# A 32-byte pad among the constants and 16 unused matmuls at the end of a gated attention and feed-forward kernel

## The chip, the core and the metric

The kernel runs on one core of one Trainium2 chip. The metric is the device time of one execution in microseconds (us). Three runs of the kernel before took 501.36, 501.48 and 502.06 us; the median is 501.48 us.

The core's engines appear as PE (TensorE, matmuls), PEld (the weight loads of TensorE), DVE (VectorE), ACT (ScalarE), POOL (GpSimd) and SP (SyncE, which issues the DMAs here). A name with a q (SPq, PEldq) is the instruction queue of that engine.

## The reference

For 4 batches and 8 heads with 768 steps and head size 48, a state of 48 x 48 is decayed and grown step by step, and read out with q. The 3072 x 384 result goes through two matrix products with an activation between them.

```python
def _attn_ref(q, k, v, alpha):
    for t in range(S):
        state = alpha[:, :, t, :, None] * state + np.einsum('bhd,bhe->bhde', k[:, :, t], v[:, :, t])
        y[:, :, t] = np.einsum('bhd,bhde->bhe', q[:, :, t], state)

def _moe_ref(x, w_in, w_out):            # x: 3072 x 384, w_in: 384 x 2048, w_out: 2048 x 384
    h = x @ w_in
    g = np.where(h >= 1, h, np.where(h <= -1, 0.0, (h + 1) ** 2 / 4.0))
    return g @ w_out
```

## The kernel before

**Attention.** The 3072 tokens are cut into 24 chunks of 128 (one batch, all heads). For a chunk `prepare` loads its decays, keys, queries and values, runs two scans on DVE (lines 478 and 485: running products forwards and backwards) and scales keys and queries with them. `attend` then issues the small matmuls of the chunk: scores (line 589), state updates (line 602), outputs (line 769).

**Feed-forward.** Three chunks make a group of 384 tokens, so there are 8 groups. A group passes through 16 slices of 128 hidden units. For a slice, `hidden` multiplies the group by `w_in` (lines 878 and 887), applies the activation on ACT (line 918, two passes) and DVE (line 928), and splits the result into a high part (ACT, line 937) and a remainder (DVE, line 938). `second` multiplies by `w_out` and accumulates in PSUM (lines 960 and 969). The first group is done in plain fp32 (lines 878 and 960); the other seven in fp32r, each product as three: high x high, high weight x remainder, remainder weight x high. That makes nine matmuls of 128 x 128 weights by 384 columns for each of `hidden` and `second`, and 7 x 16 x 9 = 1008 of them on each of the lines 887 and 969.

**Order.** All of this is recorded as operations, and `Plan.order` sets the order on each engine from modelled durations and due times. Its result is emitted inside `tc.manual_schedule()`, so the order is fixed by the code. What comes after that block, the check at the end, is placed by the framework's scheduler.

**The check at the end** (lines 1047 to 1064). Small values that POOL saved for every chunk (`meet`) are compared with bounds on DVE, counted by a matmul with a vector of ones (line 1054), summed to one number (line 1056) and turned into `flag` (line 1058). Every engine loads `flag` into a register (line 1064) and branches on it (line 1065) to a slow path that is not taken here. After the branch SP waits for the last transfers, all engines meet at a barrier, and the program ends.

**Memory.** The constants are allocated one after the other in SBUF, each rounded up to 32 bytes, then the weights, then the pools of working tiles. In the built program `zeros`, `ident`, `mask` and `both` start at multiples of 128 bytes, `raw_kq` and `fwd` at 64 past one, `state` and `meet` at 64. All 18 weight tiles `wt`, and `xs`, `w`, `Q`, `ks`, `other`, `gf`, `ot` and `gh`, start at 96 past a multiple of 128. The two buffers of `pre` start at 96 and 0, those of `inv` at 32 and 64.

Of the kernel before, what the change touches and what calls it, by code (L numbers as in the profile page):

```python
# [8 lines left out]
F32 = mybir.dt.float32  # L9
# [23 lines left out]
LAG = 4.0  # L33
# [208 lines left out]
def gated_attention_ffn(ctx: ExitStack, tc: tile.TileContext, q, k, v, alpha, w_in, w_out, by, out):  # L242
    nc = tc.nc
    B, H, S, D = q.shape
    DM, DF = H * D, w_in.shape[0] * w_in.shape[3]
    P = 128
    G = H // 2
    KT = DM // P
    NF = DF // P
# [6 lines left out]
    one = lambda name, shape, dt=F32: const.tile(shape, dt, name=name)  # L256
    zeros = one("zeros", [P, P], BF16)
# [3 lines left out]
    ident, mask = one("ident", [P, P]), one("mask", [P, P])  # L261
    both = one("both", [P, NV, 2, 2, G, 64])
    half_b, ones = one("half_b", [P, 1]), one("ones", [P, 1])
    nothing = zeros[:, None, :].broadcast_to([P, 4, P])
    with tc.manual_schedule():
        nc.vector.memset(zeros, 0.0)
# [6 lines left out]
            out=mask, in_=mask, compare_op=ALU.is_ge, fill=0.0, base=0, pattern=[[1, P]], channel_multiplier=-1  # L273
# [10 lines left out]
    wout = lambda f, a: wo[f // NW]()[:, a, f % NW]  # L284
# [11 lines left out]
    segs = [(n, 0, NF) for n in range(NG)]  # L296
# [7 lines left out]
    with ExitStack() as main:  # L304
        plan = Plan(lambda n: fill(n))
        plan.pool("wt", 2 * NU + MORE)
        pools = {}
# [559 lines left out]
        def hidden(n, f, key):  # L867

            L = groups[n] * CH
            h = bank("ps_h", 2, [P, L])  # L870
            gf = buf("fw", "gf", [P, L], 3)
            whole = n < WHOLE

            def product():
                m = 0
                for kt in range(KT):
                    if whole:
                        nc.tensor.matmul(  # L878
                            out=h(),
                            lhsT=raw_in(f)[:, kt],  # L880
                            rhs=whole_x(n)[:, kt].rearrange("p j t -> p (j t)"),
                            start=kt == 0,
                            stop=kt == KT - 1,
                        )
                        continue
                    for w, a in ((0, 0), (0, 1), (1, 0)):
                        nc.tensor.matmul(  # L887
                            out=h(),
                            lhsT=win(f, w)[:, kt],
                            rhs=xs[n]()[:, 0 : groups[n], kt, a],  # L890
                            start=(m == 0),
                            stop=(m == 3 * KT - 1),
                        )
                        m += 1

            u = f // NW
            needs = [xs[n], *([*[("x", first[n] + c) for c in range(groups[n])], raws_w[u][0]] if whole else [("moved", n), wi[u]])]

            firsts[:] = [
                plan.op(  # L900
                    "PE",
                    (0.145 + 9 * L / 2400) * (1.2 if whole else 1.0),
                    key,
                    product,
                    needs,
                    [h],
                    mode="full",
                    after=firsts,
                )
            ]  # L910


            w = L / 384
            act = lambda in_, func, scale, bias: plan.op(
                "ACT",
                0.1 + 0.45 * w,
                key + 0.4,
                lambda: nc.scalar.activation(out=gf(), in_=in_(), func=func, scale=scale, bias=bias),  # L918
                [h, gf] if in_ is gf else [h],
                [gf],  # L920
            )
            act(h, AF.Relu, 0.5, half_b)
            act(gf, AF.Square, 1.0, 0.0)
            plan.op(
                "DVE",
                0.1 + 0.45 * w,
                key + 0.4,
                lambda: nc.vector.scalar_tensor_tensor(  # L928
                    out=gf(), in0=gf(), scalar=1.0, in1=h(), op0=ALU.min, op1=ALU.max
                ),  # L930
                [gf, h],
                [gf],
            )
            if whole:
                return gf
            gh = buf("fw", "gh", [P, 2, L], 3, F32R)
            plan.op("ACT", 0.08 + 0.41 * w, key + 0.4, lambda: nc.scalar.copy(out=gh()[:, 0], in_=gf()), [gf], [gh])  # L937
            sub = lambda e: e.tensor_tensor(out=gh()[:, 1], in0=gf(), in1=gh()[:, 0].bitcast(F32), op=ALU.subtract)  # L938
            plan.op("DVE", 0.08 + 0.45 * w, key + 0.4, lambda: sub(nc.vector), [gf, gh], [gh], port=True)
            return gh  # L940
# [8 lines left out]
        def second(seg, f, gh, key):  # L949
            n, f0, f1 = seg  # L950
            L = groups[n] * CH
            if f == f0:
                o_ps[seg] = [bank("ps_o", KT, [P, L]) for _ in range(KT)]

            whole = n < WHOLE

            def product(ms):
                for m in ms:
                    if whole:
                        nc.tensor.matmul(  # L960
                            out=o_ps[seg][m](),
                            lhsT=raw_out(f)[:, m * P : (m + 1) * P],
                            rhs=gh(),
                            start=f == f0,
                            stop=f == f1 - 1,
                        )
                        continue
                    for i, (w, a) in enumerate(((0, 0), (0, 1), (1, 0))):
                        nc.tensor.matmul(  # L969
                            out=o_ps[seg][m](),  # L970
                            lhsT=wout(f, w)[:, m * P : (m + 1) * P],
                            rhs=gh()[:, a],
                            start=(f == f0 and i == 0),
                            stop=(f == f1 - 1 and i == 2),
                        )

            ms = range(KT)

            for part in [[m] for m in ms] if f == f1 - 1 else [ms]:
                plan.op(  # L980
                    "PE",
                    (0.049 + L / 800) * len(part) * (1.2 if whole else 1.0),
                    key,
                    lambda part=part: product(part),
                    [gh, raws_w[f // NW][1] if whole else wo[f // NW]],
                    [o_ps[seg][m] for m in part],
                    mode="full",
                )
            if f < f1 - 1:
                return  # L990
            w = L / 384
            for m in ms:
                ps, ot = o_ps[seg][m], buf("fw", "ot", [P, L], KT)
                plan.op(
                    "ACT",
                    0.08 + 0.37 * w,
                    key,
                    lambda ps=ps, ot=ot: copy("ACT", ot(), ps()),
                    [ps],
                    [ot],  # L1000
                    other=("DVE", 0.08 + 0.44 * w, lambda ps=ps, ot=ot: copy("DVE", ot(), ps()), False),
                )
                r0 = first[n] * CH
                plan.op(
                    "SP",
                    Plan.ISSUE,
                    key,
                    lambda m=m, r0=r0, ot=ot: nc.sync.dma_start(
                        out=out[m * P : (m + 1) * P, r0 : r0 + L], in_=ot()
                    ),  # L1010
                    [ot],
                    [],
                    moved=P * L * 4,
                )
# [10 lines left out]
        at = 0  # L1025

        for j in range(NCH):
            n = group_of[j]
            since = begin[n - 1] if n > 0 else begin[n] - AHEAD
            due = since + (begin[n] - since) * (j - first[n] + 1) / groups[n] - (MARGIN, MARGIN0, MARGIN1)[n + 1 if n < 2 else 0]  # L1030
            prepare(j, due - PREPARE + off("p", j))
            attend(j, due + off("t", j))
            done = j if j < MERGE or j == NCH - 1 else j - 1
            while at < len(segs) and first[at] + groups[at] - 1 <= done:
                if at == WHOLE:
                    for u in range(NU):
                        parts_of(u)
                for f in range(NF):
                    key = begin[at] + f * step[at]
                    second(segs[at], f, hidden(at, f, key), key + LAG)  # L1040
                at += 1
        with tc.manual_schedule():
            for o in plan.order():
                o.emit()


        near = pools["att"].tile([P, G, P], F32, name="ks", bufs=1)[:, 0, 0 : NCH * G]
# [3 lines left out]
            out=near, in0=m, scalar=1.0 + SLACK, in1=near, op0=ALU.is_le, op1=ALU.mult  # L1051
        )
        ps = pools["ps"].tile([P, 512], F32, name="ps", bufs=8)[0:1, 0 : NCH * G]
# [191 lines left out]
```

## Time and profile before

| | |
|---|---|
| median of three runs | 501.48 us (501.36 to 502.06) |
| profiled execution | span 499.7 us from the first to the last instruction; no other time of it is recorded |
| PE busy | 491.5 us, 98% of the span |
| PEld busy | 446.5 us, 89% |
| DVE, ACT, POOL busy | 347.3, 317.9 and 30.5 us |
| the two groups of 1008 matmuls | 197.1 us (line 969) and 193.6 us (line 887) |
| granted TensorE clock | full in the whole table by slices |

The busy time of PE is the union of overlapping matmuls: a matmul of 384 columns lasts some 340 ns, but the next one starts long before its end. What a matmul costs is therefore read from the length of a run of them, divided by their number.

### The profile page before, as it was taken

To read this page: it belongs to the slowest core of one execution; us is meant where nothing else is said; L and a number is where in the kernel's file an instruction comes from. 1 tells how busy PE (TensorE), PEld (TensorE's weight loads), DVE (VectorE), ACT (ScalarE), POOL (GpSimd) and SP (SyncE) were. 2 spreads that over 40 slices of the span, in tenths; PEclk is the share of its full clock that TensorE was granted. 3 is DMA by queue.
4 is the path that set the end of the run, shared out by engine and by line. 5 is a ranking of instruction groups with operands and counts; after the bars stand their busy time and mean duration, and the time that the engine had idled before them with its cause. 6 is when DMAs were issued, how large, how long until landed. Compare 5 with 4: busy or idle time off the path is not lost.

```text
span 499.7 us, 11372 instructions
## 1 busy us (share of the span) xinstructions
PE 491.5 (98%) x4586; PEld 446.5 (89%) x4586; DVE 347.3 (69%) x609; ACT 317.9 (64%) x603; POOL 30.5 (6%) x70
## 2 busy tenths in 40 slices
PE   8899999999999999999999999999999999999996
PEld 3665656699999999999999999999999999999995
DVE  6998999998997866865866857767755635343332
ACT  3799998998765565565665655665565655555551
POOL 4211102211000000000000000000000000000000
PEclk9999999999999999999999999999999999999999
DMA  8999916878552531542434513434313201001001
GB/s 315 394 387 387 330 23 142 208 201 181 181 159 65 187 102 49 150 137 82 110 95 118 174 47 124 130 100 139 115 35 89 70 1 25 1 7 42 0 1 51
DMA packets 43336, 64.42 MB, mean 129 GB/s; under 512 B 21392, under 2 KB 30736, under 8 KB 43280
## 3 DMA queue, kind: packets, MB, share of 16 engines
q1 hardware_dynamic: 41840, 59.71, 37.4%
q0 software_dynamic: 1440, 3.93, 4.2%
q8 instruction: 38, 0.62, 0.5%
q14 instruction: 18, 0.15, 0.1%
HBM read 48.56 MB, written 9.18 MB: 116 GB/s over the span
## 4 chain that ended last, share of the span: by engine, by line
PE 94%; DVE 3%; issue 1%; DMA 1%; POOL 0%; ACT 0%; DVEq 0%
PE ps L969 36%; PE ps L887 35%; PE ps L878 6%; PE ps L960 6%; PE ps L769 5%; PE ps L602 3%; PE ps L589 2%; DVE inv L485 1%; DVE pre L478 1%; DMA raw_a<-in_al 1%; PE ps L574 1%; DVE inv L493 0%; DVE Q L709 0%; DVE Q L510 0%; DVE state L653 0%
## 5 line engine op out<-in xcount | busy, mean ns | idle before, releaser
L969 PE MATMUL ps<-gh,wt 128*128 128x384 f32 x1008 | 197.1, 340 | 0.0
L887 PE MATMUL ps<-xs,wt 128*128 128x384 f32 x1008 | 193.6, 335 | 0.0
L969 PEld LDWEIGHTS ps<-gh,wt 128*128 128x128 f32 x1008 | 177.7, 188 | 1.3 <-issue 0.2
L887 PEld LDWEIGHTS ps<-xs,wt 128*128 128x128 f32 x1008 | 176.7, 188 | 0.7
L928 DVE SCALAR_TENSOR_TENSOR gf<-gf,ps 128x384 f32<-128x384 f32 x128 | 70.6, 552 | 94.0 <-ACT gf L918 92.5
L918 ACT ACTIVATE gf<-ps,half_b 128x384 f32<-128x384 f32 x128 | 74.4, 582 | 83.4 <-PE ps L887 80.5
L937 ACT CAST gh<-gf 128x384 fp32r<-128x384 f32 x112 | 57.4, 513 | 59.0 <-DVE gf L928 49.7
L938 DVE TENSOR_TENSOR gh<-gf,gh 128x384 fp32r<-128x384 f32 x112 | 62.0, 555 | 33.3 <-ACT gh L937 32.6
L918 ACT ACTIVATE gf<-gf 128x384 f32<-128x384 f32 x128 | 67.2, 525 | 4.0
L635 ACT COPY both<-state 48x192 f32<-48x192 f32 x88 | 30.8, 350 | 10.5 <-PE ps L602 9.1
L960 PE MATMUL ps<-gf,wt 128*128 128x384 f32 x96 | 33.0, 488 | 0.4 <-PE ps L878 0.4
L878 PE MATMUL ps<-xs,wt 128*128 128x384 f32 x96 | 32.7, 489 | 0.1
L478 DVE TENSOR_TENSOR_SCAN pre<-raw_a,fwd 128x516 f32<-128x516 f32 x24 | 29.5, 1228 | 3.0 <-DMA raw_a<-in_al 2.7
L485 DVE TENSOR_TENSOR_SCAN inv<-raw_a,bwd 128x516 f32<-128x516 f32 x24 | 30.1, 1254 | 2.1
L769 PEld LDWEIGHTS ps<-Q,both 128*64 128x64 f32 x368 | 23.2, 138 | 7.2 <-issue 5.6
L960 PEld LDWEIGHTS ps<-gf,wt 128*128 128x128 f32 x96 | 18.0, 190 | 12.4 <-PE ps L878 0.8
L878 PEld LDWEIGHTS ps<-xs,wt 128*128 128x128 f32 x96 | 17.8, 190 | 11.9 <-ACT wt L357 0.4
L769 PE MATMUL ps<-Q,both 128*64 128x64 f32 x368 | 26.6, 225 | 0.0
L769 PE MATMUL ps<-other,both 128*64 128x64 f32 x368 | 26.6, 225 | 0.0
L501 POOL COPY meet<-inv 128x4 f32<-128x4 f32 x24 | 9.8, 408 | 258.3 <-DVE inv L485 258.3
L769 PEld LDWEIGHTS ps<-other,both 128*64 128x64 f32 x368 | 23.2, 138 | 0.0
L709 DVE TENSOR_TENSOR Q<-ps,mask 64x256 f32<-64x256 f32 x48 | 20.3, 423 | 3.6 <-ACT other L672 1.8
(62 smaller groups left out, 370.1 us busy)
## 6 DMA issues: line engine op xcount, KB each, us to landing
raw_kq<-in_kq SPq DMA_DIRECT2D x24, 512.0 KB, 5.2
both<-in_vl SPq DMA_DIRECT2D x24, 512.0 KB, 4.6
raw_a<-in_al SPq DMA_DIRECT2D x24, 258.5 KB, 3.3
wt<-in_w_out SPq DMA_DIRECT2D x8, 768.0 KB, 9.4
wt<-in_w_in SPq DMA_DIRECT2D x8, 768.0 KB, 8.4
out<-ot SPq DMA_DIRECT2D x24, 192.0 KB, 3.1
turned<-w SPq DMA_DIRECT2D x17, 256.0 KB, 2.2
ks<-turned SPq DMA_DIRECT2D x68, 64.0 KB, 2.6
```

Of the source, the lines that this page charges most:

```text
L478: lambda: nc.vector.tensor_tensor_scan(flat(pre()), a[:, 0:n], flat(fwd), 0.0, ALU.mult, ALU.max),
L485: lambda: nc.vector.tensor_tensor_scan(flat(inv())[:, ::-1], a[:, 1 : n + 1][:, ::-1], flat(bwd)[:, ::-1], 0.0, ALU.mult, ALU.max),
L635: lambda r=r, to=to: nc.scalar.copy(out=to, in_=state[low[r], b]),
L769: nc.tensor.matmul(out=ps()[halves[r], to, halves[u]], lhsT=lhsT[:, u, r], rhs=x()[:, g, halves[u]], start=m + u == 0, stop=True, skip_gro ...
L878: nc.tensor.matmul(out=h(), lhsT=raw_in(f)[:, kt], rhs=whole_x(n)[:, kt].rearrange("p j t -> p (j t)"), start=kt == 0, stop=kt == KT - 1,)
L887: nc.tensor.matmul(out=h(), lhsT=win(f, w)[:, kt], rhs=xs[n]()[:, 0 : groups[n], kt, a], start=(m == 0), stop=(m == 3 * KT - 1),)
L918: lambda: nc.scalar.activation(out=gf(), in_=in_(), func=func, scale=scale, bias=bias),
L928: lambda: nc.vector.scalar_tensor_tensor(out=gf(), in0=gf(), scalar=1.0, in1=h(), op0=ALU.min, op1=ALU.max),
L937: plan.op("ACT", 0.08 + 0.41 * w, key + 0.4, lambda: nc.scalar.copy(out=gh()[:, 0], in_=gf()), [gf], [gh])
L938: sub = lambda e: e.tensor_tensor(out=gh()[:, 1], in0=gf(), in1=gh()[:, 0].bitcast(F32), op=ALU.subtract)
L960: nc.tensor.matmul(out=o_ps[seg][m](), lhsT=raw_out(f)[:, m * P : (m + 1) * P], rhs=gh(), start=f == f0, stop=f == f1 - 1,)
L969: nc.tensor.matmul(out=o_ps[seg][m](), lhsT=wout(f, w)[:, m * P : (m + 1) * P], rhs=gh()[:, a], start=(f == f0 and i == 0), stop=(f == f1 ...
```

## The change

One constant of 32 bytes, `pad`, is allocated behind `ones`. It is never used. Everything that is allocated behind it moves up by 32 bytes: `wt`, `xs`, `w`, `Q`, `ks`, `other`, `gf`, `ot` and `gh` now start at multiples of 128. Not every tile does: `raw_kq` stays at 64, `state` and `meet` are at 96, the two `pre` at 0 and 32, the two `inv` at 64 and 96.

Behind the planned work, still inside the fixed order, PE gets 16 matmuls whose result nobody reads: in fp32r four of 512 columns with 128 weight columns, four of 512 columns with 32 weight columns, four of 256 columns with 128 weight columns, and in bf16 four of 512 columns on zeros.

```diff
     half_b, ones = one("half_b", [P, 1]), one("ones", [P, 1])
+    one("pad", [P, 8])
     nothing = zeros[:, None, :].broadcast_to([P, 4, P])
...
                 for f in range(NF):
                     key = begin[at] + f * step[at]
-                    second(segs[at], f, hidden(at, f, key), key + LAG)
+                    last_g = hidden(at, f, key)
+                    second(segs[at], f, last_g, key + LAG)
                 at += 1
         with tc.manual_schedule():
             for o in plan.order():
                 o.emit()
+
+            gl = last_g().rearrange("p a t -> p (a t)")
+            wl = wout(NF - 1, 0)
+            rest = pools["ps"].tile([P, 512], F32, name="ps", bufs=8)
+            for L, M in ((512, P), (512, 32), (256, P)):
+                for _ in range(4):
+                    nc.tensor.matmul(out=rest[0:M, 0:L], lhsT=wl[:, 0:M], rhs=gl[:, 0:L], start=True, stop=True)
+            for _ in range(4):
+                nc.tensor.matmul(out=rest, lhsT=zeros, rhs=nothing, start=True, stop=True)
```

Up to the last 40 microseconds every engine has the same instructions in the same order, with line numbers one higher. The end is different. These are the last rows of PE before the branch, in the kernel before; line 969 is `second`, line 1054 the counting matmul of the check.

```order
L969 MATMUL ps<-gh,wt 128x384 x9
L887 MATMUL ps<-xs,wt 128x384 x9
L969 MATMUL ps<-gh,wt 128x384 x19
L1054 MATMUL ps<-ks,ones 1x96
L969 MATMUL ps<-gh,wt 128x384 x17
L1064 TENSOR_LOAD flag
L1065 COMPARE_AND_BRANCH
```

The same place of PE in the changed kernel, where lines 1053 and 1055 are the new matmuls and the counting matmul has line 1065:

```order
L970 MATMUL ps<-gh,wt 128x384 x36
L1053 MATMUL ps<-gh,wt 128x512 x4
L1053 MATMUL ps<-gh,wt 32x512 x4
L1053 MATMUL ps<-gh,wt 128x256 x4
L1055 LDWEIGHTS zeros
L1055 MATMUL ps<-zeros 128x512
...
L1065 MATMUL ps<-ks,ones 1x96
L1075 TENSOR_LOAD flag
L1076 COMPARE_AND_BRANCH
```

The counting matmul has moved from between the last products to behind all of them and behind the 16 new ones.

The end of SP's queue before, where line 1008 stores a part of the result:

```order
L827 DMA xs<-xs 16x3x256 x6
L1008 DMA out<-ot 128x384 x3
L1064 TENSOR_LOAD flag
L1064 ISA x2
L1008 DMA out<-ot 128x384 x3
L1065 COMPARE_AND_BRANCH
```

The same place of SP in the changed kernel:

```order
L828 DMA xs<-xs 16x3x256 x6
L1009 DMA out<-ot 128x384 x6
L1075 TENSOR_LOAD flag
L1076 COMPARE_AND_BRANCH
L1111 COMPARE_AND_BRANCH
```

All six last stores now stand ahead of the load of `flag`, and the two small instructions (ISA) that check the loaded value have moved behind the branch. On DVE the three last copies to `ot` likewise stand ahead of the two instructions that make `flag`.

## Rows read from the trace of the kernel before

**Rows 1.** The profile page: span, the chain's shares by line, the clock.

```profile
span 499.7 us, 11372 instructions
PEclk9999999999999999999999999999999999999999
PE ps L969 36%; PE ps L887 35%; PE ps L878 6%; PE ps L960 6%; PE ps L769 5%; PE ps L602 3%; PE ps L589 2%; DVE inv L485 1%; DVE pre L478 1%; DMA raw_a<-in_al 1%; PE ps L574 1%; DVE inv L493 0%; DVE Q L709 0%; DVE Q L510 0%; DVE state L653 0%
```

**Rows 2.** The chain of waits from 485 us: start, us, piece.

```profile
485.26 1.59 PE ps L969 x9
486.85 1.56 PE ps L887 x9
488.41 3.35 PE ps L969 x19
491.76 0.26 PE ps L1054 x2
492.01 3.20 PE ps L969 x17
495.24 0.56 DVE ot L330
```

**Rows 3.** Chain of waits at 46 us; timeline and line 1020 from 9.3 us.

```profile
46.14 5.80 PE ps L878 x18
...
9.34 3.19 PE L1020 MATMUL ps<-zeros 128*128 128x512 bf16 x14
...
L1020 PE MATMUL ps<-zeros x14: 379/379/389, 9.3 to 12.2; 128*128 128x512 bf16 x14
```

**Rows 4.** Weight loads by line and shape: busy us, mean ns, idle before.

```profile
L969 PEld LDWEIGHTS ps<-gh,wt 128*128 128x128 f32 x1008 | 177.7, 188 | 1.3 <-issue 0.2
L769 PEld LDWEIGHTS ps<-other,both 128*64 128x64 f32 x368 | 23.2, 138 | 0.0
L589 PEld LDWEIGHTS ps<-Q,inv 48*64 48x64 f32 x768 | 13.7, 134 | 1.1 <-issue 0.9 <-DVE Q L510 0.2
L769 PEld LDWEIGHTS ps<-other,xs 128*64 128x64 f32 x48 | 3.1, 138 | 0.0
L1054 PEld LDWEIGHTS ps<-ks,ones 128*1 128x1 f32 x2 | 0.1, 80 | 0.2 <-issue 0.2
```

**Rows 5.** Instructions of line 478: ns min/median/max, first and last start.

```profile
L478 DVE TENSOR_TENSOR_SCAN pre<-raw_a,fwd x24: 1223/1226/1234, 3.8 to 362.1; 128x516 f32<-128x516 f32 x24
```

**Rows 6.** PEld's waits in the first 60 us: total, times, longest.

```profile
PEld ps L878 <- ACT wt L357: 0.4, 1, 0.4
```

**Rows 7.** Timeline of the end, DVE and SP's queue.

```profile
492.05 0.24 DVE L1056 TENSOR_REDUCE total<-ps 1x1 f32<-1x96 f32 x1 [0.69 <-PE ps L1054]
492.33 0.14 DVE L1058 TENSOR_SCALAR flag<-total 1x1 int32<-1x1 f32 x1
494.77 1.39 SPq L1008 DMA_DIRECT2D out<-ot  x3
```

**Rows 8.** Instructions of lines 1064, 1065 and 1240: ns min/median/max, first, last start.

```profile
L1064 SPq TENSOR_LOAD <-flag x1: 482/482/482, 492.5 to 492.5; - x1
L1064 SPq FUSED_REGOPS  x1: 188/188/188, 493.0 to 493.0; - x1
L1064 SPq SEQ_ASSERT  x1: 29/29/29, 493.3 to 493.3; - x1
L1065 SPq EVENT_SEMAPHORE  x8: 17/17/17, 496.7 to 498.0; - x8
L1065 PEldq COMPARE_BRANCH  x1: 3382/3382/3382, 493.1 to 493.1; - x1
L1065 SPq COMPARE_BRANCH  x1: 45/45/45, 496.2 to 496.2; - x1
L1240 SPq EVENT_SEMAPHORE  x14: 17/28/28, 498.1 to 499.7; - x14
L1240 SPq DRAIN  x3: 7/7/7, 498.9 to 499.2; - x3
```

## The prediction

> **What bounds the kernel now.** I read the page first. Of the chain that ended last, 36% and 35% of the span are the matmuls of lines 969 and 887, four more lines of PE give another 20%, and the clock is full [rows 1]. So, behind a short start-up with scans on DVE, only two things can move the end: what one matmul costs PE, and what stands behind the last one.
>
> The chain of waits gives the first. In the steady part a block of nine matmuls of line 887 takes 1.56 us, 173 ns each, and one of line 969 takes 1.59 us, 177 each [rows 2]. Is that the streaming of 384 columns? Other rows say no. Eighteen plain fp32 matmuls of the same shape, which stream each column in two steps, take 5.80 us in the chain, 322 ns each, or 161 ns for one pass. Fourteen bf16 matmuls of 512 columns span 3.19 us, of which the last is seen for its whole 0.38, so they come every (3.19 - 0.38) / 13 = 216 ns, the same 0.42 ns per column [rows 3]. So 161 ns of the 173 are columns, and 12 ns are something else. The weight load of such a matmul lasts 188 ns, one of 64 columns 138, one of a single column 80 [rows 4]: 80 ns, and some 0.85 ns per column. Loads of 188 ns that follow each other at 173 ns fill PEld without a gap, and I take the load, not the columns, as what sets 173 (177 where line 969 begins with two waits).
>
> **The change, part one: 32 bytes.** Weights, products and working tiles move from 96 past a multiple of 128 bytes to a multiple. Could a load or a stream get faster? The trace holds the comparison already. Line 769 takes its weights from `both`, which lies at a multiple of 128, and for some outputs from `xs`, at 96: both loads last 138 ns. Line 589 loads `inv`, which is at 32 or 64 and then one element further, in 134 ns [rows 4]. The fp32 stream of rows 3 reads `xs` at 96 and keeps the rate of the bf16 stream that reads `zeros` at 0. On DVE the 24 scans of line 478 write `pre` alternately at 96 and at 0 and all take 1223 to 1234 ns [rows 5]. So my value is 0. As bounds, the 138 against 138 is exact to 1 ns for 64 columns, so under 2 ns for 128: 2016 x 2 = 4 us either way as the far end.
>
> [...]
>
> Transfers into `wt` and `xs` now start on rounder addresses. Only the first loads of weights could matter, since later ones lie beside a busy PE: there PEld waits once, 0.4 us, for ACT's decoding of a weight [rows 6]. Bounds: 0.4 us gained, or as much lost; I take 0.
>
> [...]
>
> **Part two: the end.** Before, the counting matmul stands between the last products. It costs PE the break: from 488.41 to 495.21 the chain holds 36 matmuls of line 969 in 6.80 us; at 1.59 us per unbroken nine they need 6.36 [rows 2]. So the products end 0.44 us earlier, at 494.77. The copies of `ot` and the last stores go with them.
>
> Then PE runs the sixteen new matmuls. None waits for another engine: they read `gh`, weights and zeros that are there. Their spacing is the longer of columns and load. For 512 columns the columns decide, 216 ns, whether 128 or 32 weights are loaded: eight, 1.73 us. For 256 columns the columns need 108 ns and the load 173, so 173 decides; by the rows it could lie between 108 and 188. With the change of shape ahead and behind: three at 0.17 and one, beside the short load of the bf16 matmul, at about 0.14: 0.66 us. Four in bf16, 0.86 us. The ends follow each other as the starts do. The counting matmul ended 0.26 after the matmul ahead of it [rows 2]. So it ends at 494.77 + 1.73 + 0.66 + 0.86 + 0.26 = 498.28.
>
> Nothing hides what follows. Before, the same chain ran from 492.02 on, under the products and the last stores. Now it ends last. From the end of the counting matmul to the load of `flag` on SP are 0.48 us (the sum on DVE at 492.05, `flag` at 492.33, the load at 492.5) [rows 7, 8]. The load takes 0.48, the branch starts 0.06 later, and 0.5 after its start (496.2 to 496.7) SP is in the next block. Eight semaphore instructions stand there. Before, they waited until 498.0 for the last store; the last of these was issued by 496.16 [rows 7]; 0.44 earlier it lands by 497.6, so now they take their bare spacing. Twelve such in the last block take 498.1 to 498.9, 0.067 each, so 0.55. The two checks of the loaded value, which ran early before, come next: 0.32 from 493.0. Then the last block and the barrier, 498.1 to 499.7, as before: 1.58 [rows 8].
>
> Sum: 498.28 + 0.48 + 0.48 + 0.06 + 0.50 + 0.55 + 0.32 + 1.58 = 502.25 us against a span of 499.7: plus 2.55 us. PE's own branch took 3.38 us before, until 1.3 us after its last matmul; even 1.3 us from the branch itself would end at 500.6 and be earlier than SP. The median of the runs is 1.8 us above the span; those 1.8 us I leave as they are. 501.48 + 2.55 = 504.0 us.
>
> The bounds of this part: if the 256-column matmuls run at their columns and no type change costs anything, 0.35 us less; if each of the two changes of type costs the 0.2 us for which PEld stood idle ahead of the counting matmul [rows 4], and the branches 0.5 more, 0.9 us more. So 503.7 to 504.9, 0.25 us wider at each end for the runs.
>
> **The rivals.**
>
> *The new addresses speed up the weight load.* For it speaks that 128 columns lie in 512 bytes, and that such a run at 96 past touches five blocks of 128 bytes instead of four. If a load paid by these, a fifth of its column part (188 - 80 = 108 ns) would be 22 ns; the columns stop the gain at 161, so 12 ns x 2016 = 24 us, and the time is 480. It starts to decide at 2.55 / 2016 = 1.3 ns per matmul, where it pays for the end; at 1.8 ns the kernel is faster by over 0.2%. Against it: 138 against 138 on line 769.
>
> *Engines meet elsewhere in memory.* A block of line 969 takes 30 ns more than one of line 887 [rows 2], and beside both ACT and DVE write `gf` and `gh`. If that is a conflict that hangs on addresses, it can vanish or double: 112 blocks x 30 ns = 3.4 us, so 500.6 or 507.4. Against it: line 969 waits for two engines at its start, which line 887 does not.
>
> *The end stays hidden.* If the last stores and not the check set the end, as before, the earlier products even give 0.44 us back: 501.0. That needs the check to be 3 us quicker than my sum, with most of it rows of durations; only the spacing of the new matmuls is not in the trace.
>
> **How the numbers follow.** A measurement of this kernel can tell about 0.2%, 1.0 us, from no change. My forecast, no effect of the addresses and a longer end, has 0.82. The faster load has 0.05, the conflict 0.10 (half each way), the hidden end 0.03. The forecast's own range is 503.4 to 505.2; a part of the conflict and partial gains widen it to 502.7 to 505.6. Faster by over 0.2% (under 500.5): 0.05. Within 0.2%, to 502.5: the hidden end and half of the conflict, 0.08. Slower: 0.87.
>
> **What would show it.** Blocks of nine at 1.56 and 1.59 us in the steady part, and loads of 188 ns, say that the addresses do nothing; 1.5 us would prove me wrong by 20 us. At the end I expect the new matmuls at 216, 216, 173 and 216 ns; the counting matmul near 498; the load of `flag` on SP some 6.2 us later than before; and the last store landed when SP's eight semaphore instructions begin. If those still wait for a store, the sum is wrong in its choice of what ends last.

## The result and the profile after

The changed kernel is slower: 505.78 us median of four runs (505.36 to 505.94) against 501.73 of the kernel before, run beside it (501.36 to 502.06). The ratio is 1.0081, 95% interval 1.0067 to 1.0096. The direction and the place were forecast; the time of 504.0 is 1.8 us too low. The measured one lies above the forecast's own range (503.4 to 505.2) and 0.2 us above the widest (502.7 to 505.6). The change is 4.05 us between the medians, against 2.55 in the forecast. The two profiled executions differ by 4.5 us of span; the one of the changed kernel took 505.94 us, the longest of its four:

```profile
span 504.2 us, 11404 instructions
```

The chain of waits of the changed kernel answers to [rows 2] (start, us, piece; line numbers are one higher, those of the check eleven):

```profile
485.53 1.59 PE ps L970 x9
487.12 1.56 PE ps L888 x9
488.68 6.34 PE ps L970 x36
495.02 2.31 PE ps L1053 x12
497.32 0.88 PE ps L1055 x4
498.20 0.27 PE ps L1065 x2
498.48 0.02 issue
498.50 0.26 DVE total L1067
498.76 0.02 issue
498.78 0.14 DVE flag L1069
```

The blocks of nine last 1.56 and 1.59 us as before, and 36 products run unbroken in 6.34. Then come twelve of the new matmuls in 2.31 us, four in 0.88, and the count. The weight loads, grouped by shape, have not changed either, beside those of [rows 4]; behind the first bar stand busy us and mean ns, behind the second the idle time before:

```profile
L970 PEld LDWEIGHTS ps<-gh,wt 128*128 128x128 f32 x1008 | 177.8, 188 | 1.1
L1053 PEld LDWEIGHTS ps<-gh,wt 128*128 128x128 f32 x8 | 1.4, 188 | 0.3
L1053 PEld LDWEIGHTS ps<-gh,wt 128*32 128x32 f32 x4 | 0.4, 108 | 0.4
```

What the forecast did not have stands behind `flag`. These are the instructions of the load, the branch and the last block (ns min/median/max, first and last start), which answer to [rows 8]:

```profile
L1075 SPq TENSOR_LOAD <-flag x1: 479/479/479, 498.9 to 498.9; - x1
L1076 SPq EVENT_SEMAPHORE  x8: 17/17/17, 500.0 to 500.5; - x8
L1076 ACTq COMPARE_BRANCH  x1: 50/50/50, 499.5 to 499.5; - x1
L1076 SPq COMPARE_BRANCH  x1: 45/45/45, 499.5 to 499.5; - x1
L1076 PEldq COMPARE_BRANCH  x1: 3578/3578/3578, 499.6 to 499.6; - x1
L1076 PEldq EVENT_SEMAPHORE  x1: 51/51/51, 503.2 to 503.2; - x1
L1251 SPq EVENT_SEMAPHORE  x14: 17/28/1737, 500.9 to 504.2; - x14
```

All engines branch between 499.48 and 499.57. On SP and ACT that lasts 0.05 us, on PE 3.58, and only at 503.2 does PE report to the last block. One of SP's 14 semaphore instructions there lasts 1.74 us. The waits of SP's queue from 497 us name whom it waited for (total, times, longest):

```profile
SPq L1251 <- PEq L1076: 1.7, 1, 1.7
```

Between 499 and 503 us the DMA queues move nothing but instructions, among them one packet on queue 8:

```profile
q8 instruction: 1, 0.02, 1.9%
```

In the trace that packet has 16 KB, starts at 500.58, 1.02 us behind the start of PE's branch, and takes 1.2 us.

### The profile page after: what moved, and what is told of

It is laid out like the page before. It is cut to its first block, busy times and chain, and to the rows that moved or that the text cites. A ratio compares the mean times of both kernels' runs of the same rounds, so it can differ in the third digit from the quotient of the medians.

```text
span 504.2 us, 11404 instructions
## 1 busy us (share of the span) xinstructions
PE 493.7 (98%) x4602; PEld 448.5 (89%) x4602; DVE 347.9 (69%) x609; ACT 317.9 (63%) x603; POOL 30.9 (6%) x70
## 4 chain that ended last, share of the span: by engine, by line
PE 94%; DVE 3%; issue 1%; DMA 1%; POOL 0%; ACT 0%; DVEq 0%
PE ps L970 36%; PE ps L888 35%; PE ps L961 6%; PE ps L879 6%; PE ps L770 5%; PE ps L603 3%; PE ps L590 2%; DVE inv L486 1%; DVE pre L479 1%; DMA raw_a<-in_al 1%; PE ps L575 1%; PE ps L1053 0%; DVE inv L494 0%; DVE Q L710 0%; DVE Q L511 0%
## 5 line engine op out<-in xcount | busy, mean ns | idle before, releaser
L636 ACT COPY both<-state 48x192 f32<-48x192 f32 x88 | 30.8, 350 | 10.5 <-PE ps L603 9.0
```

Source lines behind the costliest of these rows:

```text
L636: lambda r=r, to=to: nc.scalar.copy(out=to, in_=state[low[r], b]),
```

## The experiments

The theory after this result: PE's branch over the slow path costs 3.4 to 3.6 us from its own start (3.38 before, 3.58 now), because in it PE waits for instructions, the 16 KB packet (1.01 us before, 1.20 now). Before, it ran under the products; now nothing covers it. The rivals: the new addresses cost something, the new matmuls do, or the branch only shows a wait for matmuls that are still running.

### The two parts apart

The pad without the matmuls, and the matmuls without the pad:

```diff
-            gl = last_g().rearrange("p a t -> p (a t)")
...
-                nc.tensor.matmul(out=rest, lhsT=zeros, rhs=nothing, start=True, stop=True)
```

```diff
-    one("pad", [P, 8])
```

> The 32-byte pad alone, without the 16 matmuls; the counting matmul stands between the last products again, as in the kernel before. Theory (the addresses do nothing; the whole loss is at the end): blocks of nine stay at 1.56 and 1.59 us and the time is that of the kernel before, 501.7 us, within 0.3 us. Rival (the addresses cost something in the start-up, where the changed kernel's profile was 0.32 us late by 36 us): 502.0 us or more, in every run. Rival of the prediction (a faster load): under 500.5 us.

> The 16 matmuls without the pad, so all tiles lie where they lay before. Theory (loss at the end): 505.7 us, as the changed kernel; the new fp32r matmuls at 229 ns for 512 columns and 117 ns for 256 although their operands start at 96 past a multiple of 128 bytes. Rival (the addresses decide what a column costs): other spacings, and another time.

Measured: the pad alone 501.22 us, ratio 0.9998 (0.9988 to 1.0007); the matmuls alone 505.81, ratio 1.0092 (1.0076 to 1.0107). The pad does nothing that can be measured, and the matmuls, with the later place of the check that comes with them, bring the whole loss. Without the pad the new matmuls take the same 2.31 and 0.88 us in the chain. With the pad alone PE's branch is as long as with the matmuls, and costs nothing: it starts at 493.3 while the products run until 495.4 (first line), and it ends at 496.9, before the last store has landed at 498.0:

```profile
492.20 3.20 PE ps L970 x17
...
L1067 PEldq COMPARE_BRANCH  x1: 3622/3622/3622, 493.3 to 493.3; - x1
```

### Addresses and shapes by themselves

66 instead of 16 matmuls with 128 weight columns: five sets of six with 384 columns, five with 512, each set with both operands starting 0, 32, 96, 4 or again 0 bytes further, and six in bf16 with 384.

```diff
+            for L in (384, 512):
+                for s in (0, 8, 24, 1, 0):
+                    for _ in range(6):
+                        nc.tensor.matmul(out=rest[:, 0:L], lhsT=wl[:, s : s + P], rhs=gl[:, s : s + L], start=True, stop=True)
```

> Pad and, in place of the 16 matmuls, 66: for 384 and then 512 columns, six each with weights and columns that start 0, 32, 96, 4 and again 0 bytes past a multiple of 128; then six of 384 columns in bf16 on zeros. Theory (addresses do nothing; fp32r costs more per column whatever the load): 173 ns for 384 and 229 for 512 columns at every start, 162 for the bf16 ones. Rival (a start off a multiple of 128 costs): more than 173 and 229 at 32, 96 and 4.

From the starts in the trace, 384 columns come every 176, 175, 175, 179 and 176 ns, 512 columns every 233, 233, 234, 236 and 233, bf16 with 384 columns every 162.5. That is one execution. Its 384 columns lie 2 to 3 ns above the expected 173 at the starts 0, 32 and 96 alike. The chain of waits holds the same mean, 12.30 us / 60 = 205 ns:

```profile
494.50 12.30 PE ps L1054 x60
506.81 0.99 PE ps L1056 x6
```

A start at 96 costs nothing against one at 0 (175 against 176 ns, 234 against 233), a start off by 4 bytes 2 to 4 ns (179 and 236). The faster load of the prediction falls. So does the conflict, which the pad alone tests: its blocks still take 1.58 and 1.56 us.

### A branch with a near target

The changed kernel, with the second part of the slow path (its matrix products, which never run on these data) left out, so that PE jumps over 30 instructions and not 350 (counted in the program's listing, where an fp32r matmul is one entry; the trace has two records for it, weight load and matmul):

```diff
-        with tc.For_i(0, B * S, P) as r:
...
-                in_=whole.rearrange("m (b c t) -> m b c t", b=B, t=P)[:, b],
-            )
```

> The changed kernel with the second part of the slow path (its matrix products, which are not run here) left out of the program; some 300 instructions of TensorE less lie between the branch and its target. Theory (TensorE's branch takes 3.58 us because its target lies far behind it, and that is now the last thing to end): the branch takes under 0.7 us, as on the other engines with shorter stretches to jump over (0.18 on ScalarE, 0.5 on SyncE), SyncE's wait of 1.74 us goes, and the time is 505.7 - 1.7 = 504.0 us. Rival (the branch is as slow whatever it jumps over, because TensorE's own queue makes it so): 3.5 us and 505.7.

And with half of its inner loop, 206 entries to jump over:

```diff
-            for f in range(NF):
+            for f in range(NF // 2):
...
-                            stop=(f == NF - 1 and i == 2),
+                            stop=(f == NF // 2 - 1 and i == 2),
```

> The changed kernel with half of the slow path's matrix products left out of the program (they are not run): 206 instructions of TensorE lie between the branch and its target, against 350 in the changed kernel and 30 in the short one. If the branch's time grows with the distance: about 1.9 us. If it is one fetch of instructions that is either needed or not: 3.5 us or 0.3 us, with a 16 KB packet on the instruction queue in the first case alone.

Measured: 503.41 us with the short path, ratio 1.0039 (1.0024 to 1.0055), span 501.7; 505.51 with half of it (one execution), span 503.8. PE's branch in the first:

```profile
L1076 PEldq COMPARE_BRANCH  x1: 223/223/223, 499.2 to 499.2; - x1
```

From 499 to 503 us no packet on queue 8 is left there, only queue 14:

```profile
q14 instruction: 2, 0.02, 1.5%
```

In the second the branch, the packet and the wait of SP's queue are as with the whole path (the branch's row, the packet's, then the wait):

```profile
L1076 PEldq COMPARE_BRANCH  x1: 3658/3658/3658, 499.0 to 499.0; - x1
```

```profile
q8 instruction: 1, 0.02, 2.0%
```

```profile
SPq L1251 <- PEq L1076: 1.8, 1, 1.8
```

So between these three the branch does not pay by distance: it takes 3.66 us over 206 entries, 3.58 over 350 and 0.22 over 30, with a 16 KB packet in the first two and none in the third. The traces say so more closely still. In the nine of this case in which PE's branch has the whole or the half slow path to jump over, a 16 KB packet starts 0.95 to 1.09 us after the branch and takes 1.01 to 1.51 us, and each time the branch is 2.37 to 2.42 us longer than its packet: the longer the packet, the longer the branch. In the four with the short path there is no such packet, and the branch lasts 0.22 us.

The span of the changed kernel is 2.5 us shorter with the short path: 1.71 for SP's wait for PE, 0.32 because the products happened to end that much earlier, 0.29 since SP's own branch too gets to its next block sooner (0.19 instead of 0.48), and 0.19 for three semaphore instructions fewer.

That the branch waits for the packet is my reading of these times. From which distance on the packet comes, between 30 and 206 entries, no run shows.

### The check last, without the matmuls

The pad, no new matmuls, and the check written into the fixed order behind the products, so that its branch starts when PE has nothing left to do.

```diff
             for o in plan.order():
                 o.emit()
-        near = pools["att"].tile([P, G, P], F32, name="ks", bufs=1)[:, 0, 0 : NCH * G]
+            near = pools["att"].tile([P, G, P], F32, name="ks", bufs=1)[:, 0, 0 : NCH * G]
...
```

> The pad, none of the 16 matmuls, but the check written into the fixed order behind the products, so that the counting matmul comes after all 36 of them. Theory (what costs is that the branch starts late, and it takes 3.4 to 3.6 us from its start): products end at 494.8, counting matmul at 495.0, load of flag done at 496.2, branch done at 499.8, SyncE's last steps 1.05 us more: span 500.9, time 502.8 us. Rival (the prediction's own term: 1.3 us from the last matmul or from the branch's start, SyncE last): span 499.3 to 499.5, time 501.3 us. If the 16 matmuls themselves were the whole loss: 501.3 too.

Measured: 503.69 us, ratio 1.0048 (1.0033 to 1.0063), span 501.8. The branch lasts 3.42 us although the last matmul ended at 496.15, a microsecond before it began, so it is not a wait for matmuls; and SP waits for it as in the changed kernel (the branch's row, then SP's wait):

```profile
L1066 PEldq COMPARE_BRANCH  x1: 3418/3418/3418, 497.2 to 497.2; - x1
```

```profile
SPq L1241 <- PEq L1066: 1.6, 1, 1.6
```

The time is 0.9 us above what I expected, because DVE's two comparisons of the check had moved behind the products with it, which I had not counted. They stand in the chain of waits between the last product and the count, whose end at 496.15 is that of the last matmul:

```profile
495.27 0.21 DVE ks L1050
495.48 0.02 issue
495.50 0.27 DVE ks L1051
495.77 0.04 issue
495.81 0.34 PE ps L1055 x2
```

### The check early, and the count without TensorE

Can the end be had for less? First, the changed kernel with the check ahead of the 16 matmuls, left to the scheduler:

```diff
-            gl = last_g().rearrange("p a t -> p (a t)")
...
         near = pools["att"].tile([P, G, P], F32, name="ks", bufs=1)[:, 0, 0 : NCH * G]
...
+        with tc.manual_schedule():
+            gl = last_g().rearrange("p a t -> p (a t)")
...
```

> Pad and all 16 matmuls, but the check is written ahead of them and left to the scheduler, so the counting matmul stands between the products as in the kernel before; flag is loaded at 492.5 us again. Theory (the loss is the late check with its branch behind it, not the 3.2 us that the 16 matmuls take of TensorE): TensorE's branch of 3.4 us runs beside the last matmuls, which end at 498.5, and SyncE ends as before or 0.3 us later: 501.4 to 501.9 us. Rival (the matmuls' own time counts): 501.4 + 3.2 = 504.6 us.

Second, the kernel before with the count made by DVE and a small transfer, so that it no longer breaks the products:

```diff
-        ps = pools["ps"].tile([P, 512], F32, name="ps", bufs=8)[0:1, 0 : NCH * G]
-        nc.tensor.matmul(out=ps, lhsT=ones, rhs=near, start=True, stop=True)
+        col = pools["fw"].tile([P, 1], F32, name="col", bufs=1)
+        nc.vector.tensor_reduce(out=col, in_=near, axis=mybir.AxisListType.X, op=ALU.add)
+        row = pools["fw"].tile([1, P], F32, name="row", bufs=1)
+        nc.sync.dma_start(out=row, in_=col)
         total = pools["fw"].tile([1, 1], F32, name="total", bufs=1)
-        nc.vector.tensor_reduce(out=total, in_=ps, axis=mybir.AxisListType.X, op=ALU.add)
+        nc.vector.tensor_reduce(out=total, in_=row, axis=mybir.AxisListType.X, op=ALU.add)
```

> The kernel before with the count of the check made without TensorE: a sum along each partition on VectorE, a small DMA that turns the column into a row, a sum of that. TensorE's products run unbroken. Theory: the break of 0.44 us goes, and the end moves with the products: 501.4 - 0.4 = 501.0 us, which 5 rounds may just tell from the kernel before. Rival (something else at the end takes its place): 501.4.

Both missed what I expected. The check early takes 502.88 us, ratio 1.0033 (1.002 to 1.0046); the count without TensorE 502.91, ratio 1.0023 (1.0015 to 1.0032), though its products end at 494.75, 0.46 us earlier than before. One of its twelve runs took 500.73 us, the others 502.24 to 503.09; that one was not traced. In both kernels the wait at SP's eight semaphore instructions behind the branch, where it waits for the last stores, grew from 1.4 to 2.9 and 3.1 us. First the kernel before, then the check early, then the count without TensorE (waits of SP's queue):

```profile
SPq L1065 <- SPq L1065: 1.4, 3, 0.8
```

```profile
SPq L1078 <- SPq L1078: 2.9, 3, 2.0
```

```profile
SPq L1067 <- SPq L1067: 3.1, 3, 2.4
```

The stores are late because their packets are. In the count without TensorE these moved from 497.9 us on, 2.2 us behind the last issue:

```profile
q1 hardware_dynamic: 9, 0.01, 2.7%
```

A store has 144 packets, so nine are a sixteenth of it, the share of one of the 16 DMA engines that the profile counts, if all carry the same. They follow directly on a 16 KB packet of instructions that ran from 496.46 to 497.93. That it ran on the engine of the nine is inferred from the count and the times; the trace names queues and not engines. I took the collision for the cause, and the next three kernels test it. In the check early PE's branch counts as well: it ends 0.7 us after the last matmul, and PE reports at 498.9:

```profile
L1078 PEldq EVENT_SEMAPHORE  x1: 51/51/51, 498.9 to 498.9; - x1
```

Where SP waits for PE last, 0.99 us pass from the end of that report to the end of the program (in the changed kernel, the matmuls alone, the check last and the half path alike). So by estimate the branch alone would put the end at 499.9 us; the late stores put it at 501.0.

### The same two, and the kernel before, with the near target

Each with the second part of the slow path left out, as above; the diff is that one.

> The kernel before with the count of the check made without TensorE (as in the run before with that count, 502.91) and with the second half of the slow path, which never runs on these data, left out, so that the branches have a near target. Theory (the last stores land 1.3 us late there because instruction packets of 16 and 8 KB fall into their time; with a near target none is fetched): the last store lands by 498.0 or earlier, 500.7 to 501.1 us, that is 0.4 to 0.8 under the kernel before. Rival (the small transfer of the count, or the earlier products themselves, make the stores late): 502.7 to 503.0 as with the whole slow path.

> The kernel before with the second half of the slow path, which never runs on these data, left out; nothing else changed. Theory (the long branch of PE was hidden under products there, and its packets came after most of the stores): PE's branch falls from 3.4 us to 0.2, and the end moves by 0 to 0.5 us at most, 500.9 to 501.5. Rival (the fetch was already on the path that ended last before): 1 us or more faster, 500.4 or less.

> The pad, the check ahead of the 16 new matmuls and left to the scheduler (502.88 with the whole slow path), and the second half of the slow path, which never runs on these data, left out. Theory (stores late by the instruction packets): the last store lands by 498.0, 501.0 to 501.6 us, the 16 matmuls hidden. Rival (the new matmuls behind the products hold up the end by something else): 502.5 to 503.0 again.

Measured: the check early 501.13 us, ratio 0.9993 (0.9983 to 1.0003), as the theory had it, 1.75 less than with the whole path, of which by the estimate above about 1.0 is the stores' and 0.8 that of PE's shorter branch; the count without TensorE 501.34, ratio 0.9994 (0.998 to 1.0008), 1.57 less, but 0.2 above my expectation; the kernel before 501.73, ratio 1.0007 (0.9998 to 1.0016), no change, 0.2 above it. In the check early no store packet is left from 497.05 us on, and SP waits for PE's last matmuls instead (the queues from 497.05 to 500 us, then SP's waits):

```profile
q14 instruction: 1, 0.01, 0.7%
```

```profile
SPq L1196 <- PEq L1078: 1.1, 1, 1.1
```

In the other two one packet of 8 KB still fell among the stores, and again nine packets were late. For the count without TensorE, the queues from 497.9 us on, then SP's waits:

```profile
q1 hardware_dynamic: 9, 0.01, 2.4%
```

```profile
SPq L1185 <- DMA out<-ot: 2.0, 1, 2.0
```

Over all thirteen traces, from the end of the last store's issue to the end of its last packet:

| instruction packets among the last stores | kernels | us | packets late |
|---|---|---|---|
| none, or begun in the last 0.15 us | before, changed, pad alone, matmuls alone, addresses, check last, short path, half path, check early with short path | 1.19 to 1.25 | 0 |
| one of 8 KB | before with short path, count without TensorE with short path | 1.90, 2.18 | 9, 9 |
| one of 16 KB, two of 8 KB | check early, count without TensorE | 2.88, 3.09 | 18, 9 |

So the near target gives back the 1.4 us by which the two kernels of the last section lay above the kernel before, and in all thirteen traces store packets are late where an instruction packet began well ahead of the stores' end, and nowhere else. The trace of the count without TensorE with the short path is of an execution of 501.90 us, the longest of its eleven, so its lateness need not be that of the others.

In the two kernels with one 8 KB packet the edit did something that its diff does not show: SP's branch now stands ahead of the third store. SP branches at 495.5, runs five semaphore instructions, and issues that store at 496.15 and 496.21, each time 0.54 us after its copy was done on DVE; in the kernel before it follows 0.02 us after the copy. The rows of the kernel before with the short path (in the last, 496.2 is the start of the third store):

```profile
L1065 SPq COMPARE_BRANCH  x1: 50/50/50, 495.5 to 495.5; - x1
L1065 SPq EVENT_SEMAPHORE  x5: 17/17/17, 495.7 to 496.0; - x5
L1008 SPq DMA_DIRECT2D out<-ot x24: 332/370/1176, 100.8 to 496.2; - x24
```

Half a microsecond sooner, its packets would by estimate have been through at 497.2, about when the 8 KB packets began (497.11 and 497.39). That this order is why the two stayed above my expectation is likely, but no run separates it. None of the versions is measurably faster than the kernel before.

## Why the prediction was right, and where it failed

**Addresses: right.** Value 0, measured 501.22 against 501.4 us; blocks and loads kept their times to 0.01 us and 1 ns. PEld's wait for the decoding of a weight, 0.4 us before, is 0.3 with the pad alone and 0.4 in the check last, which has the pad too, so the 0.4 us that rounder transfers might have gained were not seen.

**The break of the count: right.** 36 products in 6.34 us, forecast 6.36. They end at 495.02 and not at 494.77; in the other kernels with this order they end between 494.46 (half of the slow path) and 494.85 (matmuls alone), so it is scatter of the runs.

**The new matmuls: the sum right, its terms wrong.** Forecast 1.73 + 0.66 + 0.86 = 3.25 us, measured 2.31 + 0.88 = 3.19. But by the starts in the trace 512 columns came every 229 ns with 128 weight columns and every 232 with 32 (forecast 216), and 256 columns every 117 ns (forecast 173), while their loads still last 188 ns. That the sum came out is luck: the two misses nearly cancel. So "I take the load, not the columns, as what sets 173" is wrong: 188 ns loads followed each other at 117. The spacings 117, 173 and 229 differ by 56 ns for each 128 columns, which is 5 ns and 0.4375 ns per column; the bf16 matmuls differ by 53.5 ns (162.5 and 216). Of the 12 ns that I could not place among the 173, 10.5 are what fp32r takes longer than bf16 at 384 columns. The 161 ns came from half of plain fp32's 322. But the trace before has 96 matmul records on line 878, two for each of the kernel's 48 matmuls there, so the two steps are two records, the eighteen of [rows 3] are nine matmuls, and 322 ns is what one step took, 0.84 ns per column. That halves it once too often; 161 stands on the 0.42 ns per column of bf16 alone. The fp32 stream then did not keep the rate of the bf16 stream, and what tests 96 against 0 are the pad alone and the shifted starts. The rival of a faster load was weaker than I thought: since loads of 188 ns did not set even 117, a quicker one would by estimate have gained nothing at 173.

**SP's own path to the end: right.** From the count's end (498.47) to the last block forecast 2.39 us, measured 2.45 (500.92); the last block without its wait 1.57 of the 1.58. Without the wait the span would be 504.2 - 1.71 = 502.5, against 502.25 in the forecast.

**PE's branch: the step that failed.** The prediction said "PE's own branch took 3.38 us before, until 1.3 us after its last matmul; even 1.3 us from the branch itself would end at 500.6 and be earlier than SP". I had taken most of the 3.38 us for a wait on running matmuls, and only the 1.3 us behind the last of them for the branch. The check last shows 3.42 us with no matmul running, and the short path 0.22 with no 16 KB packet. The row [rows 8] had the price. It was hidden, and I asked what it cost there instead of what it would cost uncovered. With the forecast's own branch at 499.30 (498.28 + 0.48 + 0.48 + 0.06), its 3.38 us and the 1.10 us that the changed kernel shows from the branch's end to the program's, the span is an estimated 503.8 and the time 505.5; with the measured wait of SP for PE, 502.25 + 1.7, they are 503.9 and 505.7. The measured time is 505.78.

**The rivals.** The hidden end (501.0) fell: SP's eight semaphore instructions now run at their bare spacing from 500.0 on, and the last store landed at 497.5. What would have kept it hidden is the check early with a near target, 501.13.

## What to carry to other kernels

When a change uncovers an instruction that ran under other work, price it from its own start at its full recorded length (here 3.38 us), on every engine that runs it, and not by the piece that stuck out before (here 1.3). The branch at this program's end was such an instruction: deciding it early, over a skipped path cut short, gave 501.13 us against 505.78. Look also at where the instruction packets fall among the last stores, which were up to 1.9 us late here. And before a load is taken as what sets a matmul's spacing, two shapes with the same load and other columns tell it apart (here 117 and 229 ns beside loads of 188).

## What the runs showed of the hardware that was not expected

- PE's branch lasted 0.22 us where it jumped over 30 instructions of the listing (four traces), and 3.4 to 3.9 us over 206 or 350 (nine). In the second case a 16 KB packet of instructions started some 1.0 us after it and took 1.0 to 1.5 us, and the branch lasted 2.37 to 2.42 us longer than the packet. SP, ACT, POOL and DVE branched at the same place in 0.05 to 0.07 us, and were at their next instruction 0.17 to 0.6 us after the start.
- Matmuls in fp32r took 0.4375 ns for a further column, those in bf16 0.418 ns (the differences 56 and 53.5 ns over 128 columns), at the full granted clock (1.00 from 494 to 499 us). The kernel with shifted operands has 57 to 59 ns for fp32r, 0.45 to 0.46 ns per column.
- Weight loads that are recorded with 188 ns did not hold back matmuls of 256 columns, which came every 117 ns; three such loads overlap in the trace (starts at 496.70, 496.82 and 496.94).
- Where instruction packets of 8 or 16 KB fell among the last stores, nine of a store's 144 packets or twice nine came late, the last of them by 0.7 to 1.9 us, and SP waited for them (four traces; none was late in the other nine).
